# Reading the weights of a one-token decoder layer in longer runs and over all 128 partitions

## Chip, cores, metric

One core of one Trainium2 chip runs the whole layer. The time is the device time of one execution in microseconds (us). The profile's span is some 2 us shorter than that time, because it starts at the first and ends at the last recorded work.

A ratio is the mean time of one kernel's fast runs over that of the other's fast runs of the same rounds, so it is not quite the ratio of the medians that are quoted.

## The reference

```
x = A_x                                        # [4, 1, 576], bf16
h  = x + attention(layernorm(x))               # 32 heads, 16 K/V heads of 128, last 4096 cached keys
out = h + mlp(layernorm(h))                    # gate, up: 576 x 4608, ReLU-gated product, down: 4608 x 576

q = xn @ wq                                    # wq: 576 x 4096
p = softmax(q k^T / sqrt(128)); o = p v        # per batch and head
attention = o.reshape(4, 1, 4096) @ wo         # wo: 4096 x 576
```

Only 4 tokens go through, so every byte of the weights and of the cache is used about once: 134 MB of K and V, 25 MB of weights.

## The kernel before

An own small scheduler keeps a list of operations for each engine and turns dependencies into semaphore waits. All loads are issued by SyncE, in the order in which the data are needed: the first K tile, wq, K and V tiles of 2 MB in a ring of 8 slots, then wo, gate and up, W_down. `place` makes a load wait for the last reader of the SBUF region that it overwrites. PE transposes K, multiplies scores and V; at the end come the wo product, a layernorm with the feature dimension on partitions, the gate/up product, and W_down.

576 features are 4 chunks of 128 and a last chunk of 64. The weights were loaded like this:

```
def add_wq(m):
    ...
    if m < 2:                                   # 256 rows, two per partition: runs of 16 KB
        src = A_wq[m * 256:(m + 1) * 256, :].rearrange("(p r) n -> p (r n)", r=2)
        ...
    else:                                       # the last 64 rows: 64 partitions
        place(("wq", m), off, TILE, "QMM",
              lambda e: e.dma_start(out=arena[0:64, off:off + H * DH], in_=A_wq[512:576, :]), key=f"slot{s}")
...
place(("wo",), WO_OFF, H * D, "WO",             # row h*128+p to partition p: 4096 runs of 1152 B
      lambda e: e.dma_start(out=arena[:, WO_OFF:WO_OFF + H * D].rearrange("p (h n) -> p h n", n=D),
                            in_=A_wo.rearrange("(h p) n -> p h n", p=128)))
...
for c in range(DC):                             # chunks of 128 rows, the last of 64: runs of 9 KB
    w = _dw(c)
    for g, W in ((0, B_W_gate), (1, B_W_up)):
        ...
        place(("gu", g, c), off, F, ("GU", c),
              lambda e, off=off, w=w, W=W, c=c: e.dma_start(out=arena[0:w, off:off + F], in_=W[c * 128:c * 128 + w, :]))
...                                             # W_down: four loads of 9 rows per partition
```

The attention output is turned so that partition p holds element p of every head, which is the order of wo above:

```
pe(("OT", b), lambda e: e.matmul(m_ps[:, 0:32], lhsT=o_sb[:, :], rhs=selw[:, 0, :], start=True, stop=True), ...)
```

Of the kernel before, what the change touches and what calls it, by code (L numbers as in the profile page):

```python
# [6 lines left out]
ALU = mybir.AluOpType  # L7
AX = mybir.AxisListType
FP32 = mybir.dt.float32
BF16 = mybir.dt.bfloat16  # L10

B = 4
D = 576
# [21 lines left out]


def _dw(c):
    return 128 if c < 4 else 64
# [85 lines left out]
def bass_sequential_preLN__sliding_block_cached__glu_gated_reglu__decode_kernel(  # L124
# [12 lines left out]
    with ExitStack() as es:  # L137
# [19 lines left out]
        ind = sb("ind", [128, 32], FP32)  # L157
# [4 lines left out]
        xn_bf = sb("xn_bf", [B, D], BF16)  # L162
        bn = sb("bn", [B, 2, 6], FP32)
        mv = sb("mv", [B, 8], FP32)
        xnT = sb("xnT", [128, DC, 32], BF16)
# [7 lines left out]
        selw = sb("selw", [128, 2, 32], FP32)  # L173
        rL = sb("rL", [128, 32], FP32)
        o_sb = sb("o_sb", [128, 128], FP32)
        oT = sb("oT", [128, H, 32], BF16)
        hnT = sb("hnT", [128, DC, 32], BF16)
        R_sb = sb("R_sb", [128, 2, DC, B], FP32)
# [7 lines left out]
        g_sb = pflat[:, 1152:1152 + 2304].bitcast(FP32)  # L186
        hh = pflat[:, 3456:3456 + 1152]
        hhT = pflat[:, 4608:4608 + 1152]
# [46 lines left out]

        wq_off = []

        def add_wq(m):
            s = ring_slot()
            off = slot0 + s * TILE  # L240
            if m < 2:
                wq_off.extend([off, off + H * DH])
                src = A_wq[m * 256:(m + 1) * 256, :].rearrange("(p r) n -> p (r n)", r=2)
                place(("wq", m), off, TILE, "QMM", lambda e: e.dma_start(out=arena[:, off:off + TILE], in_=src), key=f"slot{s}")
            else:
                wq_off.append(off)
                place(("wq", m), off, TILE, "QMM",
                      lambda e: e.dma_start(out=arena[0:64, off:off + H * DH], in_=A_wq[512:576, :]), key=f"slot{s}")
# [17 lines left out]
        for n, v in enumerate(rest):  # L266
            add_kv("V", v)
            if n == len(rest) - 4:
                place(("wo",), WO_OFF, H * D, "WO",
                      lambda e: e.dma_start(out=arena[:, WO_OFF:WO_OFF + H * D].rearrange("p (h n) -> p h n", n=D),  # L270
                                            in_=A_wo.rearrange("(h p) n -> p h n", p=128)))
        gu_off = {}
        for c in range(DC):
            w = _dw(c)
            for g, W in ((0, B_W_gate), (1, B_W_up)):
                off = GU_OFF + (2 * c + g) * F
                gu_off[(g, c)] = off
                place(("gu", g, c), off, F, ("GU", c),
                      lambda e, off=off, w=w, W=W, c=c: e.dma_start(out=arena[0:w, off:off + F], in_=W[c * 128:c * 128 + w, :]))
        wd_off = []  # L280
        for j in range(4):
            off = WD_OFF + j * WDJ if j < 2 else WO_OFF + (j - 2) * WDJ
            wd_off.append(off)
            place(("wd", j), off, WDJ, "DOWN",
                  lambda e, off=off, j=j: e.dma_start(out=arena[:, off:off + WDJ],
                                                      in_=B_W_down[j * 1152:(j + 1) * 1152, :].rearrange("(p r) n -> p (r n)", p=128)))
# [19 lines left out]
        pool("c_ind0", lambda e: e.memset(ind[:, :], 0.0))  # L306
        prev = "c_ind0"
        for j in range(4):
            pool(f"c_ind{j + 1}", lambda e, j=j: e.affine_select(out=ind[:, :], in_=ind[:, :], pattern=[[-1, 32]],
                                                               compare_op=ALU.not_equal, fill=1.0, base=-32 * j,  # L310
                                                               channel_multiplier=1), [prev])
            prev = f"c_ind{j + 1}"
        pool("c_sel0", lambda e: e.memset(sel4[:, :], 0.0))
        pool("c_sel", lambda e: e.tensor_copy(out=sel4[:, 0:4], in_=ind[:, 0:4]), ["c_sel0", prev])
        IND = prev
        pool("c_oT", lambda e: e.memset(oT[:, :, :], 0.0))
        pool("c_hnT", lambda e: e.memset(hnT[:, :, :], 0.0))
        pool("c_R", lambda e: e.memset(R_sb[:, :, :, :], 0.0))
# [8 lines left out]
        for hf in range(2):  # L327
# [8 lines left out]

        tpv = bankb[6]
        xn_rows = lambda c: (xn_bf[0:B, 512:576] if c == 4 else
                             xn_bf[0:B, c // 2 * 256:c // 2 * 256 + 256].rearrange("b (p r) -> b r p", r=2)[:, c % 2, :])

        def pe_q():
            for c in range(DC):
                w = _dw(c)
                pe(None, lambda e, c=c, w=w: e.transpose(out=tpv[0:w, c * 4:(c + 1) * 4], in_=xn_rows(c),
                                                         identity=ident_b[0:B, 0:B]), ["xn", "c_idb"] if c == 0 else [])
            for c in range(DC):
                w = _dw(c)
                pe("TP1", lambda e, c=c, w=w: e.transpose(out=tpv[0:w, 32 + c * 4:32 + (c + 1) * 4],
                                                          in_=x_bf[0:B, c * 128:c * 128 + w], identity=ident_b[0:B, 0:B]))
            for c in range(DC):  # L350
                w = _dw(c)
                off = wq_off[c]
                for n in range(8):
                    g, bk = n % 4, n // 4
                    pe("QMM", lambda e, c=c, w=w, off=off, n=n, g=g, bk=bk: e.matmul(  # L355
                        bank[4 + bk][32 * g:32 * g + 32, :], lhsT=xnT[0:w, c, :], rhs=arena[0:w, off + n * 512:off + (n + 1) * 512],
# [9 lines left out]
        def dve_q():  # L366
            dve(None, lambda e: e.tensor_copy(out=xnT[:, 0:4, 0:4], in_=tpv[:, 0:16].rearrange("p (c b) -> p c b", b=B)), ["TP1", "c_xnT"])
            dve("xnT", lambda e: e.tensor_copy(out=xnT[0:64, 4, 0:4], in_=tpv[0:64, 16:20]))
            dve(None, lambda e: e.tensor_copy(out=xT[:, 0:4, :], in_=tpv[:, 32:48].rearrange("p (c b) -> p c b", b=B)))
            dve("xT", lambda e: e.tensor_copy(out=xT[0:64, 4, :], in_=tpv[0:64, 48:52]))  # L370
# [112 lines left out]
        def weights(b):  # L483
# [11 lines left out]
            dve(("SEL", b), lambda e: e.tensor_scalar(out=selw[:, 0, :], in0=ind[:, :], scalar1=stat[:, b, 4:5], scalar2=None,  # L495
                                                      op0=ALU.mult), [("W", b), IND])
            dve(("SELL", b), lambda e: e.tensor_scalar(out=selw[:, 1, :], in0=ind[:, :], scalar1=stat[:, b, 4:5],
                                                       scalar2=stat[:, b, 2:3], op0=ALU.mult, op1=ALU.mult), [("EXP", b)])
            pe(("LS", b), lambda e: e.matmul(m_ps[:, 0:32], lhsT=ones_h[:, :], rhs=selw[:, 1, :], start=True, stop=True),
               [("SELL", b), "c_onesh"])  # L500
            dve(("RL", b), lambda e: e.reciprocal(out=rL[:, :], in_=m_ps[:, 0:32]), [("LS", b)])

        def finish_o(b):
            dve(("OEV", b), lambda e: e.tensor_copy(out=o_sb[:, :], in_=o_ps[:, 0:DH]), [("PV", b * KVH + KVH - 1)])  # L504
            pe(("OT", b), lambda e: e.matmul(m_ps[:, 0:32], lhsT=o_sb[:, :], rhs=selw[:, 0, :], start=True, stop=True),
               [("OEV", b), ("SEL", b), ("RL", b)])
            dve(("ONORM", b), lambda e: e.tensor_tensor(out=oT[:, :, b], in0=m_ps[:, 0:32], in1=rL[:, :], op=ALU.mult),  # L507
                [("OT", b), "c_oT", ("RL", b)])
# [43 lines left out]
        act("part1", lambda e: e.copy(out=part[:, 288:576], in_=bank[1][:, 0:288]), ["WO", ("PV", NPAIR - 1)])  # L552
        for c in range(DC):
            w = _dw(c)
            pe("HT", lambda e, c=c, w=w: e.matmul(m_ps[0:w, c * 4:(c + 1) * 4], lhsT=part[:, c * 128:c * 128 + w], rhs=sel4[:, 0:4],
                                                  start=True, stop=True), ["part0", "part1", "c_sel"] if c == 0 else [])
        dve("h1", lambda e: e.tensor_tensor(out=R_sb[:, 0, 0:4, :], in0=m_ps[:, 0:16].rearrange("p (c b) -> p c b", b=B),
                                            in1=xT[:, 0:4, :], op=ALU.add), ["HT", "c_R", "xT"])
        dve("h2", lambda e: e.tensor_tensor(out=R_sb[0:64, 0, 4, :], in0=m_ps[0:64, 16:20], in1=xT[0:64, 4, :], op=ALU.add))
        dve("h3", lambda e: e.tensor_tensor(out=R_sb[:, 1, :, :], in0=R_sb[:, 0, :, :], in1=R_sb[:, 0, :, :], op=ALU.mult),  # L560
            ["h1", "h2"])
        pe("STAT", lambda e: e.matmul(bank[6][:, 0:40], lhsT=ones_d[:, :], rhs=R_sb[:, :, :, :].rearrange("p a c b -> p (a c b)"),
                                      start=True, stop=True), ["h3", "c_onesd", ("OEV", B - 1)])
        dve("s1", lambda e: e.tensor_reduce(out=st2[:, 0:8], in_=bank[6][:, 0:40].rearrange("p (s c b) -> p s b c", s=2, c=DC, b=B),
# [9 lines left out]
        dve("n1", lambda e: e.tensor_tensor(out=tmp5[:, :, :], in0=R_sb[:, 0, :, :], in1=mean_bc, op=ALU.subtract), ["s1"])  # L574
# [85 lines left out]
```

## Time and profile before

| | before |
|---|---|
| median of 3 runs | 398.67 us (398.4 to 399.05) |
| span of the profile | 396.6 us |
| bytes read | 159.58 MB, 402 GB/s over the span |
| PE busy | 65% |

In the views PE is TensorE (matmuls), PEld its loads of weights, DVE VectorE, ACT ScalarE, POOL GpSimd, and SPq SyncE's queue, which issues the loads. A packet is one entry of the DMA records; here it has the size of one run (for wo 4096 packets of 1152 B).

From the page of the kernel before: the busy share of the 16 DMA engines and their rate in 40 equal slices, and the shares of the chain of waits.

```profile
DMA  7999999999999999999999999999999999999993
GB/s 313 385 406 426 418 425 431 422 428 423 423 430 423 425 425 430 430 421 425 425 430 423 425 430 425 429 423 425 423 430 430 410 369 368 426 424 419 229 354 142
...
DMA 61%; PE 25%; SPq 6%; DVE 5%; issue 1%; ACT 1%
```

The DMA row is full from the second slice to the last but one, so the DMA engines bound the kernel, and every stretch in which a full row moves fewer bytes is a loss. The rate row shows them: slices 2 and 3 (385, 406), slices 33 and 34 (369, 368), and the dip to 229 in slice 38. The windows view of the kernel before places them. Its columns are the stretch, its length, the busy time of the five engines with their instructions, the granted clock of TensorE, the DMA share and the rate:

```profile
core 0: us, PE busy (x) PEld busy (x) DVE busy (x) ACT busy (x) POOL busy (x), PEclk, DMA share, GB/s
17.50:20.50 3.00, 1.80 (x16) 0.48 (x16) 0.00 (x0) 0.00 (x0) 0.00 (x0) 0.72 1.14 257
313.00:320.00 7.00, 2.88 (x132) 2.44 (x124) 0.00 (x0) 0.00 (x0) 0.00 (x0) 0.74 1.01 396
322.00:325.00 3.00, 1.90 (x64) 1.63 (x64) 0.00 (x0) 0.00 (x0) 0.00 (x0) 0.50 1.08 391
326.00:329.00 3.00, 0.00 (x0) 0.00 (x0) 0.00 (x0) 0.00 (x0) 0.00 (x0) 0.50 0.60 211
350.00:366.00 16.00, 11.45 (x186) 7.52 (x178) 2.58 (x13) 0.60 (x2) 0.00 (x0) 0.68 1.01 424
367.00:372.00 5.00, 0.67 (x12) 0.23 (x12) 0.00 (x0) 0.00 (x0) 0.00 (x0) 0.84 1.04 225
372.00:379.50 7.50, 2.30 (x24) 0.58 (x24) 0.00 (x0) 0.00 (x0) 0.00 (x0) 0.50 0.99 217
388.30:392.20 3.90, 0.75 (x36) 0.56 (x36) 0.00 (x0) 0.00 (x0) 0.00 (x0) 0.83 0.46 190
```

The stretch at 350 us is the normal rate. Around 19 us come wq's last 64 rows, from 367 to 379.5 us the last 64 rows of gate and up: the DMA share is 1 and the rate is about half (the first window is a little wider than its stretch). From 313 us half of the engines read wo and the others still V tiles, at 396 GB/s; with all 16 on wo, from 322 us, the rate is 391. In 326 to 329 us half of the engines have nothing to do (DMA share 0.60, 9.6 packets in flight). The view of SyncE's own timeline shows that the loads behind wo were issued late:

```profile
305.27 0.39 SPq L270 DMA_DIRECT2D sb_arena<-in_A_wo_dram  x1
305.71 24.04 SPq L233 DMA_DIRECT2D sb_arena<-in_A_v_cache_dram  x3
```

wo is issued at 305.27 us. The three V tiles behind it take 24.04 us to issue. The end, in PE's timeline of the kernel before (the bracket is the idle time before the group and what ended it):

```profile
385.95 2.00 PE L622 MATMUL psb<-sb_arena,sb_pTm 128*32 128x144 bf16 x72
389.62 0.75 PE L622 MATMUL psb<-sb_arena,sb_pTm 128*32 128x144 bf16 x36 [1.67 <-DMA sb_arena<-in_B_W_down_dram]
392.71 1.27 PE L622 MATMUL psb<-sb_arena,sb_pTm 128*32 128x144 bf16 x36 [2.34 <-DMA sb_arena<-in_B_W_down_dram]
```

After the last landing at 392.7 us, 36 matmuls remain. Last, three pieces of the chain of waits in order of time (start, length, what): each ends when the last byte of that load has landed.

```profile
2.54 18.80 DMA sb_arena<-in_A_wq_dram
...
329.14 19.90 DMA sb_arena<-in_A_v_cache_dram
...
356.87 35.79 DMA sb_arena<-in_B_W_down_dram
```

So wq had landed at 21.3 us, the last V tile at 349.0 us and W_down at 392.7 us.

### The profile page before, as it was taken

The page shows a single profiled execution, that of the slowest core. Times are in us where ns is not written, and L with a number is a line of the kernel's source. Part 1 is how long each engine was busy: PE and PEld are TensorE (multiplying, and loading weights), DVE is VectorE, ACT ScalarE, POOL GpSimd, SP SyncE. Part 2 cuts the span into 40 slices and gives each one's busy share as a digit, 9 for nine tenths or more (in the row PEclk, how much of TensorE's full clock was granted, in tenths as well). Part 3 has the DMA queues.
Part 4 walks back from the last instruction along what each step waited for, and adds up shares of the span by engine and source line. Part 5 has one row for each costly group of instructions (what it writes and reads, how often), then busy time and mean ns, then how long its engine had stood idle before and what let it go on. Part 6 is the DMA issues. An engine that isn't in the chain of part 4 may idle for free.

```text
span 396.6 us, 10818 instructions
## 1 busy us (share of the span) xinstructions
PE 259.7 (65%) x5123; PEld 206.2 (52%) x5123; DVE 126.7 (32%) x228; ACT 141.3 (36%) x154; POOL 4.4 (1%) x24
## 2 busy tenths in 40 slices
PE   1647999779677768768677777777774530366153
PEld 1535777558466656557566665666653420343022
DVE  3247555734222334423223444222232100011020
ACT  3305777744344453434333634333350100000010
POOL 4000000000000000000000000000000000000000
PEclk9958999998988888987888889888895555558656
DMA  7999999999999999999999999999999999999993
GB/s 313 385 406 426 418 425 431 422 428 423 423 430 423 425 425 430 430 421 425 425 430 423 425 430 425 429 423 425 423 430 430 410 369 368 426 424 419 229 354 142
DMA packets 15668, 160.28 MB, mean 404 GB/s; under 512 B 1348, under 2 KB 5448, under 8 KB 5448
## 3 DMA queue, kind: packets, MB, share of 16 engines
q1 hardware_dynamic: 15600, 159.59, 97.5%
q8 instruction: 40, 0.66, 0.7%
q14 instruction: 4, 0.03, 0.0%
q10 hardware_dynamic: 24, 0.01, 0.0%
HBM read 159.58 MB, written 0.00 MB: 402 GB/s over the span
## 4 chain that ended last, share of the span: by engine, by line
DMA 61%; PE 25%; SPq 6%; DVE 5%; issue 1%; ACT 1%
DMA sb_arena<-in_A_k_cache_dram 34%; PE psb L397 15%; DMA sb_arena<-in_A_v_cache_dram 13%; DMA sb_arena<-in_B_W_down_dram 9%; SPq L233 6%; DMA sb_arena<-in_A_wq_dram 5%; PE psb L427 4%; PE psb L477 3%; DVE sb_pTm L525 2%; DVE sb_pTm L462 1%; PE psb L547 1%; PE psb L450 1%; ACT sb_p_sb L440 1%; DVE sb_arena L409 0%; PE psb L622 0%
## 5 line engine op out<-in xcount | busy, mean ns | idle before, releaser
L397 PE MATMUL psb<-sb_ident_b,sb_arena 128*128 128x128 bf16 x2048 | 146.7, 238 | 58.3 <-DMA sb_arena<-in_A_k_cache_dram 54.8
L411 ACT COPY sb_arena<-psb 128x1024 bf16<-128x1024 bf16 x128 | 124.9, 1014 | 138.4 <-PE psb L397 138.4
L397 PEld LDWEIGHTS psb<-sb_ident_b,sb_arena 128*128 128x128 bf16 x2048 | 134.9, 108 | 71.8 <-DMA sb_arena<-in_A_k_cache_dram 58.0
L409 DVE COPY sb_arena<-psb 128x1024 bf16<-128x1024 bf16 x128 | 88.0, 690 | 145.8 <-PE psb L397 145.7
L477 PE MATMUL psb<-sb_arena,sb_pTm 128*32 128x128 bf16 x2048 | 46.5, 246 | 36.7 <-DMA sb_arena<-in_A_v_cache_dram 32.5
L477 PEld LDWEIGHTS psb<-sb_arena,sb_pTm 128*32 128x32 bf16 x2048 | 40.5, 111 | 53.8 <-DMA sb_arena<-in_A_v_cache_dram 36.1
L427 PE MATMUL psb<-sb_arena,sb_qTm 128*32 128x512 bf16 x512 | 44.5, 426 | 1.8 <-ACT sb_p_sb L440 1.8
L589 PE MATMUL psb<-sb_arena,sb_hnT 128*32 128x384 bf16 (+1 forms) x120 | 8.7, 437 | 13.9 <-DMA sb_arena<-in_B_W_up_dram 7.3
L552 ACT COPY sb_pTm<-psb 128x288 f32<-128x288 f32 x1 | 0.4, 399 | 44.0 <-PE psb L547 44.0
L504 DVE COPY sb_o_sb<-psb 128x128 f32<-128x128 f32 x4 | 1.2, 292 | 44.3 <-PE psb L477 44.3
L589 PEld LDWEIGHTS psb<-sb_arena,sb_hnT 128*32 128x32 bf16 (+1 forms) x120 | 3.5, 117 | 18.4 <-DMA sb_arena<-in_B_W_up_dram 8.8
L427 PEld LDWEIGHTS psb<-sb_arena,sb_qTm 128*32 128x32 bf16 x512 | 8.0, 96 | 9.5 <-issue 4.1
L462 DVE TENSOR_SCALAR sb_pTm<-psb,sb_par 128x512 bf16<-128x512 bf16 x16 | 9.0, 639 | 6.0 <-PE psb L450 6.0
L440 ACT ACTIVATE sb_p_sb<-psb,sb_stat 128x2048 bf16<-128x2048 f32 x4 | 7.9, 1967 | 5.8 <-DVE sb_stat L436 5.8
L593 ACT ACTIVATE sb_pTm<-psb 128x384 f32<-128x384 f32 x3 | 1.3, 491 | 21.5 <-PE psb L589 21.5
L596 DVE TENSOR_TENSOR sb_pTm<-psb,sb_pTm 128x384 bf16<-128x384 f32 x3 | 1.5, 551 | 21.5 <-ACT sb_pTm L593 21.5
L525 DVE MEMSET sb_pTm<- 128x8192 uint32 x1 | 6.9, 6885 | 1.6 <-issue 1.6
L450 PE MATMUL psb<-sb_ident_b,sb_p_sb 128*128 128x128 bf16 x64 | 5.7, 242 | 2.5 <-DVE sb_oT L507 1.3
L494 ACT ACTIVATE sb_stat<-sb_stat 128x1 f32<-128x1 f32 x4 | 0.8, 203 | 18.0 <-DVE sb_stat L492 18.0
L622 PE MATMUL psb<-sb_arena,sb_pTm 128*32 128x144 bf16 x144 | 4.0, 285 | 4.0 <-DMA sb_arena<-in_B_W_down_dram 4.0
L355 PE MATMUL psb<-sb_arena,sb_xnT 128*32 128x512 bf16 (+1 forms) x40 | 3.9, 516 | 4.1 <-DMA sb_arena<-in_A_wq_dram 3.7
L450 PEld LDWEIGHTS psb<-sb_ident_b,sb_p_sb 128*128 128x128 bf16 x64 | 4.4, 108 | 3.5 <-DVE sb_pTm L462 1.5
(98 smaller groups left out, 66.2 us busy)
## 6 DMA issues: line engine op xcount, KB each, us to landing
sb_arena<-in_A_k_cache_dram SPq DMA_DIRECT2D x32, 2048.0 KB, 32.6
sb_arena<-in_A_v_cache_dram SPq DMA_DIRECT2D x32, 2048.0 KB, 31.0
sb_arena<-in_B_W_down_dram SPq DMA_DIRECT2D x4, 1296.0 KB, 34.1
sb_arena<-in_A_wo_dram SPq DMA_DIRECT2D x1, 4608.0 KB, 29.1
sb_arena<-in_B_W_gate_dram SPq DMA_DIRECT2D x4, 1152.0 KB, 28.7
sb_arena<-in_B_W_up_dram SPq DMA_DIRECT2D x4, 1152.0 KB, 31.0
sb_arena<-in_A_wq_dram SPq DMA_DIRECT2D x2, 2048.0 KB, 14.2
sb_arena<-in_B_W_gate_dram SPq DMA_DIRECT2D x1, 576.0 KB, 36.2
```

Of the source, the lines that this page charges most:

```text
L233: lambda e: e.dma_start(out=arena[:, off:off + TILE], in_=src), key=f"slot{s}")
L397: o = pe(("TRJ", i, j), lambda e, j=j, u=u, t=t: e.transpose(out=bankb[TRB[j]][:, u * 128:(u + 1) * 128], in_=kn[:, t, :], identity=ident_ ...
L409: dve(("EV", i, j), lambda e: e.tensor_copy(out=dst, in_=src), deps)
L411: act(("EV", i, j), lambda e: e.copy(out=dst, in_=src), deps)
L427: o = pe(("QK", i), lambda e, a=a, j=j: e.matmul(bank[4 + u][32 * j:32 * j + 32, :], lhsT=qTm[:, b, 2 * k2 + a, :], rhs=k[:, j, :, :, a], ...
L440: act(("EXP", b), lambda e: e.activation(out=p_sb[:, :].rearrange("p (k a) -> p k a", a=2), in_=bass.AP(tensor=psb, offset=4 * 512, ap=[[4 ...
L450: pe(("PT", b, r), lambda e, tl=tl: e.transpose(out=mb_ps[:, tl * 128:(tl + 1) * 128], in_=p_sb[:, (r * 8 + tl) * 128:(r * 8 + tl + 1) * 128],
L462: dve(("PM", b, r, a), lambda e, dst=dst, src=src, a=a: e.tensor_scalar(out=dst, in0=src, scalar1=par[:, a:a + 1], scalar2=None, op0=ALU.m ...
L477: pe(("PV", i), lambda e, tl=tl, j=j: e.matmul(o_ps[32 * j:32 * j + 32, 0:DH], lhsT=pTm[:, u * 8 + tl, j, k2, :], rhs=v[:, 16 * j + 8 * u ...
L525: dve("c_pTm", lambda e: e.memset(pflat, 0.0))
L589: pe(("GU", c), lambda e, c=c, w=w, g=g, m=m, j=j, lo=lo: e.matmul(bank[3 * g + m][32 * j:32 * j + 32, 0:384], lhsT=hnT[0:w, c, :], rhs=ar ...
L622: pe("DOWN", lambda e, j=j, r=r, n=n, wv=wv: e.matmul(bank[0][32 * n:32 * n + 32, 0:144], lhsT=hhT[:, r * 128 + 32 * j:r * 128 + 32 * j + 32],
```

## The change

The intent is to keep the DMA engines at their full rate over the whole run:

- the last 64 rows of wq, gate and up are cut in two halves of columns and put on 128 partitions, two partitions to a row;
- wo is read with 32 consecutive rows in one partition (36 KB runs), gate and up with two (18 KB runs);
- the activations are laid out to match: four matmuls instead of one turn the attention output, the last chunk of features is duplicated over pairs of partitions and masked by parity, and the layernorm sums count that chunk by half;
- the last load of W_down is cut into 6 and 3 rows, so that fewer matmuls wait for the last bytes.

```diff
+        def rows(W, m):
+            if m < 2:
+                return W[m * 256:(m + 1) * 256, :].rearrange("(p r) n -> p (r n)", r=2)
+            return W[512:576, :].rearrange("r (a n) -> (r a) n", a=2)
...
-                      lambda e: e.dma_start(out=arena[0:64, off:off + H * DH], in_=A_wq[512:576, :]), key=f"slot{s}")
+            place(("wq", m), off, n, "QMM", lambda e: e.dma_start(out=arena[:, off:off + n], in_=rows(A_wq, m)), key=f"slot{s}")
...
-                      lambda e: e.dma_start(out=arena[:, WO_OFF:WO_OFF + H * D].rearrange("p (h n) -> p h n", n=D),
-                                            in_=A_wo.rearrange("(h p) n -> p h n", p=128)))
+                      lambda e: e.dma_start(out=arena[:, WO_OFF:WO_OFF + H * D], in_=A_wo.rearrange("(p r) n -> p (r n)", p=128)))
...
-                      lambda e, off=off, w=w, W=W, c=c: e.dma_start(out=arena[0:w, off:off + F], in_=W[c * 128:c * 128 + w, :]))
+                      lambda e, off=off, n=n, W=W, m=m: e.dma_start(out=arena[:, off:off + n], in_=rows(W, m)))
...
+            for r0, r1 in ((0, 9),) if j < 3 else ((0, 6), (6, 9)):
...
-            pe(("OT", b), lambda e: e.matmul(m_ps[:, 0:32], lhsT=o_sb[:, :], rhs=selw[:, 0, :], start=True, stop=True),
+            for q in range(4):
+                pe(("OT", b), lambda e, q=q: e.matmul(m_ps[:, 0:32], lhsT=selw[:, q, :], rhs=o_sb[:, 32 * q:32 * q + 32],
+                                                      start=(q == 0), stop=(q == 3)),
...
+        dve("n2", lambda e: e.tensor_copy(out=hnT[:, 0:4, 0:4], in_=tmp5[:, 0:4, :]), ["n2a", "c_hnT"])
+        for a in range(2):
+            dve("n3", lambda e, a=a: e.tensor_scalar(out=hnT[:, 4 + a, 0:4], in0=tmp5[:, 4, :], scalar1=par[:, a:a + 1], scalar2=None,
+                                                     op0=ALU.mult), ["n2a", "c_hnT"])
```

(The constants, the transposes of x and the order of the gate/up matmuls are cut.)

## The prediction

> **What bounds it now.** The DMA engines. The page's DMA row is full from 3 to 390 us, at about 425 GB/s; PE is busy 65%. The chain of waits gives 61% to DMA. So the time is the sum of the transfers of the slower engines, plus a start and a tail. Three stretches (windows view) fall below 425 GB/s:
>
> - 17.3 to 20.9 us, 215 GB/s: wq's last 64 rows. Their 8 KB packets take 0.61 us each, as long as a 16 KB packet elsewhere.
> - 313 to 334 us, 390 GB/s, and 211 GB/s in 326 to 329: wo, 4096 packets of 1152 B at 0.051 us.
> - 367 to 379.5 us, 220 GB/s with all 16 engines busy: gate/up's last 64 rows.
>
> At the end, 388 to 392 us runs at 196 GB/s: half the engines are done. From wo on they run some 7 us ahead of the others.
>
> **Why 64 rows cost that much.** [...] the rate halves. It lasts 12.5 us, though 1.18 MB at 215 GB/s is 5.5 us: I think because the two halves of the engines reach these rows at different times, and each visit halves both.
>
> **Costing.** Packet durations fit 8.5 ns plus size/27.2 GB/s (1152 B 0.051, 9216 B 0.347, 16384 B 0.611 us); new sizes are estimated from that fit. Along the late half of the engines, which never idles and ends last:
>
> - wq: 3.5 us at half rate becomes full rate: -1.6 us.
> - wo: 256 packets x 0.051 = 13.1 us per engine becomes 8 rows of 36 KB, 10.9 us: -2.1 us. The hole at 326 to 329 us (SyncE's next issue was held up until 328.5 us behind wo's descriptors) hit the early half, so filling it gains nothing directly.
> - gate/up last rows: -6.2 us.
> - gate/up in 18 KB runs: per engine 64 packets of 9 KB become 32 of 18 KB, 22.2 to 22.0 us: -0.2 us.
> - Last W_down piece is cut 6 + 3 rows, so 12 matmuls remain after the last landing instead of 36 (1.30 us now): -0.8 us; +0.1 us for shorter runs.
>
> Added: four f32 matmul pairs for OT instead of one (about +0.5 us), partd, n2a/n3 and a second STAT matmul (about +1 us) on the PE/DVE chain between the last V and the gate/up matmuls; Pool constants at the start, in its idle time. That chain now ends at 360.9 us; I estimate 358.6 after. The gate/up matmuls then take 7 to 9 us, to about 367; gate/up's last landing falls near 369: still bound by DMA, with 1 to 2 us to spare. So the added work is hidden. W_down's last landing: near 381.8 us.
>
> **Sum:** -11.6 us. Predicted 387.0 us, range 384.8 to 390.5. Faster by over 2% 0.94, within 2% 0.05, slower 0.01.
>
> **What would show it.** No window at 215 GB/s with all engines busy; 4 KB and 4.6 KB packets near 0.16 and 0.18 us; no long SyncE issue behind wo; wo over in about 11 us per engine; 12 matmuls after the last landing; a one-sided DMA tail of 3 to 7 us still there.
>
> **What would make it wrong.** 36 KB runs cut into small pieces or read slower; the half rate coming from something other than the 64 rows; PE and its 0.5 clock becoming the limit after 365 us, which would eat 1 to 3 us; or the early half gaining no lead, which would gain up to 2 us more.

The terms for wq and for gate/up's last rows come from rates in the trace of before (the text's 215 to 220 GB/s, beside 424 in the window at 350 us); that 128 partitions would bring the full rate was the estimate. The sum is -11.6 us; its terms add to -10.8 us, as told at the end.

## The result

| | before | after |
|---|---|---|
| median | 398.6 us (398.4 to 399.05, 4 runs) | 388.63 us (388.57 to 388.7, 4 runs) |
| ratio | | 0.9748, 95% interval 0.9732 to 0.9765 |
| span | 396.6 us | 386.9 us |
| mean rate over the span | 402 GB/s | 412 GB/s |

The kernel is 2.5% faster, 10.0 us. The same lines of the page, of the new kernel:

```profile
DMA  7999999999999999999999999999999999999993
GB/s 307 425 430 432 430 418 427 421 427 425 429 430 422 423 427 427 425 425 425 427 427 427 429 422 420 426 427 429 425 425 427 422 447 420 417 432 425 420 380 123
...
DMA 65%; PE 25%; DVE 5%; issue 1%; ACT 1%; SPq 1%
```

The dips are gone, and the share of DMA in the chain has grown. The windows of the new kernel:

```profile
core 0: us, PE busy (x) PEld busy (x) DVE busy (x) ACT busy (x) POOL busy (x), PEclk, DMA share, GB/s
17.50:20.50 3.00, 1.66 (x24) 0.46 (x24) 0.29 (x1) 0.29 (x1) 0.00 (x0) 1.00 1.03 430
313.00:320.00 7.00, 1.64 (x88) 1.19 (x76) 0.00 (x0) 0.00 (x0) 0.00 (x0) 0.74 1.01 430
326.00:329.00 3.00, 0.00 (x0) 0.00 (x0) 0.00 (x0) 0.00 (x0) 0.00 (x0) 0.50 0.98 415
360.00:370.00 10.00, 7.02 (x100) 3.76 (x104) 0.48 (x4) 0.00 (x0) 0.00 (x0) 0.67 1.00 417
375.10:383.10 8.00, 5.04 (x144) 3.76 (x145) 0.76 (x2) 0.27 (x1) 0.00 (x0) 0.55 0.52 214
```

Around 19 us and in 360 to 370 us, where the last 64 rows now come, the rate is 430 and 417 GB/s. A new thing stands in the last line: for 8 us the DMA share is 0.52. The stretch was 3.9 us long before. Half of the engines have ended their loads by then (8 packets are in flight at 378 us, 16 at 375 us). I call them the early half, the others the late half, and the time in which only the late half still works the tail. SyncE's timeline of the new kernel:

```profile
304.06 0.33 SPq L272 DMA_DIRECT2D sb_arena<-in_A_wo_dram  x1
304.44 1.83 SPq L235 DMA_DIRECT2D sb_arena<-in_A_v_cache_dram  x3
```

The three V tiles behind wo are issued in 1.83 us. PE at the end, new kernel:

```profile
376.20 2.54 PE L650 MATMUL psb<-sb_arena,sb_pTm 128*32 128x144 bf16 x72 [0.34 <-DVE sb_pTm L634]
380.57 1.27 PE L650 MATMUL psb<-sb_arena,sb_pTm 128*32 128x144 bf16 x36 [1.83 <-DMA sb_arena<-in_B_W_down_dram]
382.62 1.61 PE L650 MATMUL psb<-sb_arena,sb_pTm 128*32 128x144 bf16 x36 [0.78 <-DMA sb_arena<-in_B_W_down_dram]
```

The third and fourth W_down pieces wait for DMA (1.83 and 0.78 us idle), so PE isn't the limit. Their last 12 matmuls start at 383.68 us, when the last 3 rows have landed. The chain of waits, new kernel:

```profile
2.52 16.98 DMA sb_arena<-in_A_wq_dram
...
305.66 40.80 DMA sb_arena<-in_A_v_cache_dram
...
356.79 26.84 DMA sb_arena<-in_B_W_down_dram
```

With the landing times of both chains, and the last landing of gate/up (380.61 and 371.27 us, from the PE work that waited for it: the first line is of the kernel before, the second of the new one), the 9.7 us of the span divide like this:

```profile
380.61 1.15 PE L589 MATMUL psb<-sb_arena,sb_hnT 64*32 64x384 bf16 x12 [1.65 <-DMA sb_arena<-in_B_W_up_dram]
371.27 0.14 PEld L617 LDWEIGHTS psb<-sb_arena,sb_hnT 128*32 128x32 bf16 x8 [0.84 <-DMA sb_arena<-in_B_W_up_dram]
```

| stretch | before, ends at | after, ends at | gain in this stretch | predicted |
|---|---|---|---|---|
| to wq landed | 21.34 | 19.50 | 1.84 | 1.6 |
| to the last V landed (contains wo) | 349.04 | 346.46 | 0.74 | 2.1 |
| to gate/up landed | 380.61 | 371.27 | 6.76 | 6.4 |
| to W_down landed | 392.66 | 383.63 | -0.31 | -0.1 |
| to the end of the span | 396.6 | 386.9 | 0.7 | 0.8 |

### The profile page after: what moved, and what is told of

Read it like the earlier page. It is cut to its first block, busy times and chain, and to the rows that moved or that the text cites. A ratio compares the mean times of both kernels' runs of the same rounds, so it can differ in the third digit from the quotient of the medians.

```text
span 386.9 us, 10877 instructions
## 1 busy us (share of the span) xinstructions
PE 263.6 (68%) x5149; PEld 211.2 (55%) x5149; DVE 128.7 (33%) x233; ACT 141.5 (37%) x154; POOL 7.2 (2%) x29
## 4 chain that ended last, share of the span: by engine, by line
DMA 65%; PE 25%; DVE 5%; issue 1%; ACT 1%; SPq 1%
DMA sb_arena<-in_A_k_cache_dram 43%; PE psb L414 16%; DMA sb_arena<-in_A_v_cache_dram 11%; DMA sb_arena<-in_B_W_down_dram 7%; DMA sb_arena<-in_A_wq_dram 4%; PE psb L444 4%; PE psb L494 3%; DVE sb_pTm L547 2%; DVE sb_pTm L479 1%; ACT sb_p_sb L457 1%; PE psb L569 1%; DVE sb_stat L451 1%; PE psb L525 0%; PE psb L467 0%; SPq L235 0%
## 5 line engine op out<-in xcount | busy, mean ns | idle before, releaser
L494 PEld LDWEIGHTS psb<-sb_arena,sb_pTm 128*32 128x32 bf16 x2048 | 41.2, 113 | 48.9 <-DMA sb_arena<-in_A_v_cache_dram 31.9
L617 PE MATMUL psb<-sb_arena,sb_hnT 128*32 128x384 bf16 x120 | 9.3, 488 | 4.7 <-DMA sb_arena<-in_B_W_up_dram 2.3
L617 PEld LDWEIGHTS psb<-sb_arena,sb_hnT 128*32 128x32 bf16 x120 | 4.3, 133 | 9.0 <-DMA sb_arena<-in_B_W_up_dram 3.6
L650 PE MATMUL psb<-sb_arena,sb_pTm 128*32 128x144 bf16 x144 | 5.3, 324 | 3.1 <-DMA sb_arena<-in_B_W_down_dram 2.6
L467 PE MATMUL psb<-sb_ident_b,sb_p_sb 128*128 128x128 bf16 x64 | 4.9, 220 | 2.9 <-DVE sb_pTm L479 1.2
L650 PEld LDWEIGHTS psb<-sb_arena,sb_pTm 128*32 128x32 bf16 x144 | 3.8, 138 | 4.4 <-DMA sb_arena<-in_B_W_down_dram 3.9
L525 PE MATMUL psb<-sb_o_sb,sb_selw 128*128 128x32 f32 x32 | 5.1, 310 | 1.6 <-DVE sb_o_sb L523 1.6
L525 PEld LDWEIGHTS psb<-sb_o_sb,sb_selw 128*128 128x128 f32 x32 | 4.7, 225 | 2.5 <-DVE sb_o_sb L523 2.5
```

The costliest lines, as they stand in the source:

```text
L467: pe(("PT", b, r), lambda e, tl=tl: e.transpose(out=mb_ps[:, tl * 128:(tl + 1) * 128], in_=p_sb[:, (r * 8 + tl) * 128:(r * 8 + tl + 1) * 128],
L494: pe(("PV", i), lambda e, tl=tl, j=j: e.matmul(o_ps[32 * j:32 * j + 32, 0:DH], lhsT=pTm[:, u * 8 + tl, j, k2, :], rhs=v[:, 16 * j + 8 * u ...
L525: pe(("OT", b), lambda e, q=q: e.matmul(m_ps[:, 0:32], lhsT=selw[:, q, :], rhs=o_sb[:, 32 * q:32 * q + 32], start=(q == 0), stop=(q == 3)) ...
L617: pe(("GU", c), lambda e, g=g, m=m, j=j, lo=lo, c=c: e.matmul(bank[3 * g + m][32 * j:32 * j + 32, 0:384], lhsT=hnT[:, c if c < 4 else 4 + ...
L650: pe("DOWN", lambda e, j=j, r=r, n=n, wv=wv: e.matmul(bank[0][32 * n:32 * n + 32, 0:144], lhsT=hhT[:, r * 128 + 32 * j:r * 128 + 32 * j + 32],
```

## The experiments

The theory to test: the DMA stream of the engines that end last is the time; 64-partition loads halve it, for longer than their own bytes need; wo's short runs cost a little; and work added to PE is hidden. Every kernel starts from the new one, and "slower" or "faster" is against its 388.63 us. Comparing medians of different chips is a risk, since the new kernel itself did not run in the experiments. ot_twice, which was expected not to differ, ran on another chip in 388.66 us, but it is itself a test. The traces support the comparison better: fewer than 14 packets are in flight from 375.1 to 375.4 us on in the new kernel, dma_only, ot_twice, less_fetch and more_fetch2 alike, on different chips. By the ratios the times on two of the chips come out 0.7 to 0.9 us lower against the new kernel (early64 +5.5 us, early128 +2.1, more_fetch2 +0.6, less_fetch -2.6).

### wo back to short runs

```diff
-                      lambda e: e.dma_start(out=arena[:, WO_OFF:WO_OFF + H * D], in_=A_wo.rearrange("(p r) n -> p (r n)", p=128)))
+                      lambda e: e.dma_start(out=arena[:, WO_OFF:WO_OFF + H * D].rearrange("p (h n) -> p h n", n=D),
+                                            in_=A_wo.rearrange("(h p) n -> p h n", p=128)))
...   (and the one OT matmul of before, with its selector, so that the result stays right)
```

> The new kernel with wo alone taken back to 4096 runs of 1152 B (with the old order of the attention output, so the result stays right). Theory A (my corrected costing: in the trace of before 17.3 of these packets are in flight on 16 engines, so one costs an engine 47 ns and not its recorded 51 ns; only the late half of the engines counts): 1.1 us slower than the new kernel, so ratio to before near 0.9775; the SyncE issue behind wo is held up for some 20 us again, a hole of about 3 us at half rate appears, and the one-sided tail shrinks from 7.7 us to about 4 us. Theory B (the costing on record, 51 ns each): 2.1 us slower, ratio 0.980. Theory C (the hole costs as well): 3.5 us or more slower, ratio 0.9835 or more.

Measured: 389.63 us, correct, ratio 0.9778 (0.976 to 0.9795). That is 1.0 us slower: theory A. SyncE's timeline of this kernel shows the blocked issue again:

```profile
303.99 24.18 SPq L236 DMA_DIRECT2D sb_arena<-in_A_v_cache_dram  x3
```

The DMA records show the hole (at 326 us 9 packets are in flight, not 16) and a one-sided tail of 3.7 us, where the new kernel has 8.05 us. So filling the hole moved half of the engines forward and moved the last ones only by the 0.9 us of wo's short runs (last load at 384.1 and 383.2 us): the hole of 3 us became 4 us more of tail.

### gate/up's last 64 rows back on 64 partitions

```diff
-                      lambda e, off=off, n=n, W=W, m=m: e.dma_start(out=arena[:, off:off + n], in_=rows(W, m)))
+                      lambda e, off=off, n=n, W=W, m=m, w=w: e.dma_start(out=arena[0:w, off:off + n],
+                                                                         in_=rows(W, m) if m < 2 else W[512:576, :]))
...   (n = F and w = 64 for m == 2; an unduplicated chunk hn64[0:64] of the normalized h as lhsT for these rows)
```

> The new kernel with only the last 64 rows of gate and up read into 64 partitions in 9 KB runs, as before. Theory A (64-partition loads halve all engines, and the two halves of the engines reach them some 7 us apart, so the half rate lasts about 12 us): 6 to 7 us slower than the new kernel, ratio near 0.991; 12 to 13 us at 215 GB/s. Theory B (64-partition loads run at half rate for their own bytes only): 2.8 us slower, ratio near 0.982, 5.5 us at 215 GB/s. Theory C (the half rate is not due to the 64 partitions): no change, ratio 0.975.

Measured: 396.13 us, correct, ratio 0.9937 (0.9921 to 0.9953): 7.5 us slower, of the 10.0 us that the whole change gained. Theory A, a little beyond its 7 us. The windows of this kernel (same columns as before) show two visits, with a recovery between them:

```profile
361.00:365.00 4.00, 3.28 (x48) 1.62 (x40) 0.00 (x0) 0.00 (x0) 0.00 (x0) 0.65 1.04 234
366.00:370.00 4.00, 0.17 (x6) 0.00 (x0) 0.00 (x0) 0.00 (x0) 0.00 (x0) 1.00 1.00 345
372.00:376.00 4.00, 2.95 (x36) 1.05 (x36) 0.00 (x0) 0.00 (x0) 0.00 (x0) 0.50 0.99 209
```

In 361 to 365 us, eight engines of the early half read the 64 rows while the others still read 128-partition rows; in 372 to 376 us it is the other way round. The sizes of the packets in flight show this. Both times the rate halves for all (234 and 209 GB/s): in the first visit the others' packets of 18432 B take about 1.25 to 1.4 us instead of 0.69, in the second W_down's packets of 10368 B about 0.76 us instead of 0.389. The lag between the halves is larger here than before the change (8 against 4 us), which fits that undoing costs 7.5 us while the change gained 6.76 us in this stretch; no run varies the lag alone.

### The same 64 rows at the start, where all engines are in step

```diff
+        for g, W in ((0, B_W_gate), (1, B_W_up)):            # after wq; early64:
+            P.dma("sync", ("L", "xtra", g), lambda e, g=g, W=W: e.dma_start(out=pflat[0:64, g * F:(g + 1) * F], in_=W[512:576, :]), f"d_xtra{g}")
                                                              # early128 instead:
+            ...  e.dma_start(out=pflat[:, g * F // 2:(g + 1) * F // 2], in_=rows(W, 2)) ...
-                dve("c_pTm", lambda e: e.memset(pflat, 0.0))
+                dve("c_pTm", lambda e: e.memset(pflat, 0.0), [("L", "xtra", 0), ("L", "xtra", 1)])
```

That they are in step there can be read from the new kernel's records: wq's last 128 packets start from 17.5 us on, 16 of them within 0.3 us, and the last 16 end between 18.86 and 19.04 us.

> The new kernel plus 1.18 MB of extra loads right after wq at the start, when all engines are in step: gate's and up's last 64 rows, read once more into 64 partitions (never used). Theory A (in step, the half rate lasts once, for these bytes alone): at 215 GB/s 5.5 us, with a run-off of about 0.8 us, so 5.5 to 6.3 us slower than the new kernel, and 2.8 to 3.5 us slower than early128. Theory B (64-partition loads always cost what they cost at the end, 12 us at half rate): 9 us or more slower than the new kernel and 6 to 7 us slower than early128.

> The same extra 1.18 MB, read into 128 partitions in 4.6 KB runs. Both theories: 2.8 us slower than the new kernel (1.18 MB at 425 GB/s), ratio to before near 0.982; no stretch at half rate.

Measured: early64 394.95 us (ratio 0.9887, 0.987 to 0.9903), early128 391.43 us (ratio 0.9801, 0.9785 to 0.9817), both correct: 6.3 and 2.8 us slower. The same 1.18 MB, 64 against 128 partitions, cost 3.5 us more in step and 7.5 us more out of step. Theory A holds. One window of early64, and the same of early128 (same columns):

```profile
19.50:24.00 4.50, 1.24 (x16) 0.57 (x16) 1.48 (x9) 0.59 (x1) 0.00 (x0) 1.00 1.04 215
```

```profile
19.50:24.00 4.50, 2.08 (x16) 0.91 (x16) 0.93 (x4) 0.59 (x1) 0.00 (x0) 0.50 1.05 438
```

### wq's last 64 rows back on 64 partitions

```diff
-            place(("wq", m), off, n, "QMM", lambda e: e.dma_start(out=arena[:, off:off + n], in_=rows(A_wq, m)), key=f"slot{s}")
+            place(("wq", m), off, n, "QMM", lambda e: e.dma_start(out=arena[0:w, off:off + n], in_=rows(A_wq, m) if m < 2 else A_wq[512:576, :]), key=f"slot{s}")
...   (n = H * DH and w = 64 for m == 2, and xnT's last chunk on 64 partitions)
```

> The new kernel with only wq's last 64 rows read into 64 partitions, as before. If the DMA stream of the whole run is shifted by what the stretch at 17 to 21 us loses: 1.6 us slower than the new kernel, ratio near 0.979. Rival: the loss at the start is absorbed later, because K tiles queue up for PE until about 100 us: under 0.4 us, ratio 0.975 to 0.976.

Measured: 390.34 us, correct, ratio 0.9799 (0.978 to 0.9817): 1.7 us slower. What is lost in the first 21 us is still missing at the end; in the page of the new kernel the DMA row is full in between. The rival falls.

### The last W_down piece in one load

```diff
-            for r0, r1 in ((0, 9),) if j < 3 else ((0, 6), (6, 9)):
+            for r0, r1 in ((0, 9),):
```

> The new kernel with the last W_down piece loaded whole (9 rows per partition). After the last landing 36 matmuls remain instead of 12: 0.7 to 0.8 us slower than the new kernel, ratio near 0.9767, the stream itself ending 0.1 us earlier. Rival: nothing, because the matmuls of the first six rows cannot run before the last landing either; ratio 0.975.

Measured: 389.25 us, correct, ratio 0.9768 (0.975 to 0.9785): 0.6 us slower, close to the expected 0.7. The interval alone would not tell it from the new kernel; that all four runs lie between 389.15 and 389.35 us does.

### Added PE work doubled

```diff
+            for rep in range(2):
                 for q in range(4):
                     pe(("OT", b), ...)
```

> The new kernel with the four matmuls of the last step of attention done twice (same result): about 1.9 us more on the chain of PE and VectorE between the last V and the gate/up matmuls at the half clock. If that chain is hidden behind the weights' DMA with 1 to 2 us to spare, as the trace of the new kernel shows: 0 to 0.4 us slower than the new kernel, ratio 0.975 to 0.976. Rival (PE already bounds the end): 1.5 to 2 us slower, ratio 0.979 or more.

Measured: 388.66 us, correct, ratio 0.973 (0.9714 to 0.9747): no slower. The half clock of the expectation is in the new kernel's trace: around these matmuls, at 348.8 to 350.8 us, the granted clock is 0.50. The largest added piece on the chain of PE and VectorE is hidden; the smaller ones (partd, n2a/n3, STAT) were not doubled.

### Which part of 64 partitions is the cost: the partitions, or the number of engines that write them

```diff
+                for p0 in (0, 1, 2, 3, 32, 33, 34, 35):      # 8 loads of 8 rows, 4 partitions apart, per matrix
+                    make = lambda e, off=off, n=n, W=W, p0=p0: e.dma_start(
+                        out=arena[p0:p0 + 29:4, off:off + n], in_=W[512 + p0:512 + p0 + 29:4, :])
...   (the rest as in gu64)
```

> The last 64 rows of gate and up go to partitions 0 to 63 again in 9 KB runs, as in gu64, but by eight loads of 8 rows each per matrix, the rows of one load 4 partitions apart[...]. Theory A[...]: no stretch at 215 GB/s. Then the eight engines carry the whole 1.18 MB, 16 packets of 0.347 us each instead of 16 of 0.178 us: if they are the early half, the late half is relieved of 2.85 us and the kernel is 2.5 to 3 us faster than the new kernel (ratio near 0.968), the one-sided tail shrinking from 7.7 to about 2 us; if they are the late half, it is 2.7 us slower (ratio near 0.982) and the tail grows to 13 us. Theory B (64 partitions run at half rate whichever engines write them): about 7.5 us slower like gu64, ratio near 0.994.

That a load of 8 rows uses eight engines was assumed; the trace fits it (below).

Measured: 391.29 us, correct, ratio 0.9817 (0.9799 to 0.9836): 2.7 us slower than the new kernel and 4.8 us faster than gu64, with the same rows on the same 64 partitions. The windows (same columns):

```profile
360.00:372.00 12.00, 6.75 (x108) 3.47 (x108) 0.59 (x5) 0.00 (x0) 0.00 (x0) 0.78 1.00 420
380.00:385.80 5.80, 2.70 (x111) 2.32 (x104) 0.00 (x0) 0.00 (x0) 0.00 (x0) 0.79 0.14 57
```

The half rate is gone (420 GB/s in the first line), so 64 partitions as such do not cost it. The trace fits eight engines: 96 of the 128 packets of 9 KB run up to six at a time, the other 32 two at a time, which is 16 for each of eight engines. So it is shown that loading these rows on fewer engines avoids the half rate, but not by what mechanism, nor why 128-partition loads on other engines halve as well in gu64. The records name no engine.

My guess that these eight engines are either the early half or the late half was wrong, although the time fits the second. In the records six packets of 9 KB are in flight at 362 to 364 us and two from 368 us on: six of the eight engines belong to the early half and two to the late one. At the end two engines alone work until 385.8 us (57 GB/s in the second line above), and they make the 2.7 us.

### Where the lag of half of the engines comes from

First the loads alone, without any compute:

```diff
-                owner[blk] = reader
+                owner[blk] = ("L",) + name        # a slot waits only for the load before it
...   (all operations of PE, VectorE, ScalarE and GpSimd removed; x copied to out)
```

> The loads of the new kernel in the same order and sizes, each slot waiting only for the earlier load into it; no compute at all, the output is wrong on purpose (a copy of x). Measures the floor of the stream and where the lead of half the engines comes from. Theory A (half of the engines move each packet a little slower, 0.62 against 0.61 us): a one-sided tail of 4 us or more stays, and the stream ends within 3 us of the new kernel's. Theory B (the lead comes from the instruction fetches, 40 of 16 KB that share the engines with the loads, and there are almost none here): the tail is under 2 us and the stream ends 4 to 7 us earlier than the new kernel's.

Measured: 380.54 us, ratio 0.9526 (0.951 to 0.9542). It passed the comparison with the reference although it computes nothing, because x is most of the output. The page of this kernel, rate in 40 slices and the loads' queue:

```profile
GB/s 308 425 436 424 432 424 432 426 432 426 432 424 432 424 432 426 432 426 431 426 429 429 424 434 422 434 424 434 422 432 426 432 443 424 418 429 429 429 417 268
...
q1 hardware_dynamic: 11384, 159.59, 99.0%
```

The last slice moves 268 GB/s where the new kernel's moves 123: there is no one-sided tail. The last 16 packets of the loads end between 375.5 and 376.6 us, about 1 us apart: no half is late. In the new kernel the early half begins to run out at 375.1 us as well, and the late half is done at 383.2 us. So something that comes with the compute delays half of the engines by 8 us and the others not at all.

The instruction fetches are the candidate: on its queue q8, of the kind "instruction", the new kernel has 40 packets of 16 KB for 10,877 instructions, one for each 272, and dma_only, with 113 instructions, has no such queue. Each stands in the records in place of a load's packet, for 1.07 us on average. Two more kernels change their number:

```diff
+                for _ in range(2 if tl < 7 else 0):          # more_fetch2; more_fetch: 5
+                    pe(None, lambda e: e.matmul(bank[6][0:32, 256:257], lhsT=ident_b[:, 0:32], rhs=ident_b[:, 0:1],
+                                                start=True, stop=True, skip_group_check=True))
```

> The new kernel with 2240 tiny matmuls of one column added among those of the V tiles, into an unused column; PE has a third of its time free, and the result stays the same. They add about 4480 PE instructions, 41% more, so some 17 more instruction fetches of 16 KB besides the 40. Theory A (the lead of half the engines comes from the fetches, which fall on the other half and cost it 42.7 us of packets plus 20 us of slowed loads for 40, 1.57 us each): the late half loses 17 x 1.57 / 8 = 3.3 us more, so 3.3 us slower than the new kernel (ratio near 0.983) and a one-sided tail of about 11 us. Theory B (the lead comes from compute engines using SBUF, not from the fetches): under 0.7 us slower, tail unchanged at 7 to 8 us. Theory C (PE becomes the limit): 5 us or more slower, with the DMA row of the page no longer full.

Measured: 418.63 us (416.39 to 420.49), correct, ratio 1.0501 (1.0467 to 1.0535). The fetches rose to 57 as counted, but PE became the limit (theory C), as the page's DMA row shows:

```profile
DMA  7999999999999999999999999989999139999990
```

The stream ran dry in slices 32 and 33 (57 and 114 GB/s), and the halves came back into step there. This run says nothing about the lag. The smaller dose:

> As more_fetch, with 896 tiny matmuls instead of 2240, so that PE should not become the limit; the result stays the same. 1792 more PE instructions, by the count of more_fetch (17 more fetches for 4480) 7 more fetches. Theory A (the fetches fall on the half that ends last, at 1.57 us each over eight engines): 1.4 us slower than the new kernel (ratio near 0.978), tail about 9 us. Theory B (the lead has another cause in the compute): under 0.4 us slower, tail as before at 7 to 8 us. Theory C (PE still limits): 3 us or more slower, DMA row with slices under 9.

Measured: 390.12 us, correct, ratio 0.9762 (0.9739 to 0.9785): 1.5 us slower. And fewer instructions:

```diff
-            for tl in range(8):
+            for tl in range(2):                              # less_fetch, V product
```

> The new kernel with only two of the eight key groups of each V tile multiplied (wrong on purpose; all loads stay). 1536 fewer matmuls, 3072 fewer PE instructions, so about 12 fewer fetches, 28 instead of 40. Theory A (the fetches make the late half late): 2.4 us faster than the new kernel, ratio near 0.969, tail near 5.5 us. Theory B (PE reading SBUF slows the loads): only the packet durations of the loads would change; theory D (nothing but PE time changes, and PE is not the limit): no change, ratio 0.974 to 0.976, tail 7 to 8 us.

Measured: 386.98 us (wrong), ratio 0.9684 (0.9661 to 0.9707): 1.65 us faster, less than the 2.4 us expected. The queue of the instruction fetches (packets, MB, share of the span of 16 engines) in the new kernel, in more_fetch2 and in less_fetch:

```profile
q8 instruction: 40, 0.66, 0.7%
```

```profile
q8 instruction: 47, 0.77, 0.8%
```

```profile
q8 instruction: 28, 0.46, 0.5%
```

Together, with times taken from the DMA records:

| kernel | fetches of 16 KB | fewer than 14 packets in flight from | last load ends | tail |
|---|---|---|---|---|
| dma_only | 0 | 375.1 us | 376.6 us | 1.5 us |
| less_fetch | 28 | 375.3 us | 381.5 us | 6.2 us |
| new kernel | 40 | 375.1 us | 383.2 us | 8.05 us |
| more_fetch2 | 47 | 375.2 us | 384.65 us | 9.45 us |

By the ratios, more_fetch2 and less_fetch are 0.8% apart, 3.1 us, as by the medians. The early half does not move; the late half moves by (384.65 - 376.6) / 47 = 0.17 us for each fetch, 1.4 us of engine time if eight engines share them evenly.

The records do not name the engines, but they hold more. In these records a packet usually starts within some 4 ns of the end of the one before it on its engine, so the packets can be linked, by times and by the known order of loads, into 16 chains of equal length, one for each engine. This linking is an inference, but it comes out without a remainder. In the new kernel the 40 fetches fall on eight chains in turn, five on each; these end at 382.8 to 383.2 us, and the eight chains without a fetch at 375.0 to 377.3 us. The other kernels tell fetches from compute as a whole, within one execution each:

| kernel | fetches on a chain | chains | their loads end |
|---|---|---|---|
| less_fetch | 3 | 4 | 379.8 to 380.0 us |
| less_fetch | 4 | 4 | 381.3 to 381.5 us |
| more_fetch2 | 5 | 1 | 383.0 us |
| more_fetch2 | 6 | 7 | 384.3 to 384.7 us |

So one more fetch makes its engine 1.4 to 1.5 us later: about 1.07 us for the fetch, and about 0.5 us because the load's packet behind it takes some 1.1 us instead of 0.61. It also tells why less_fetch gained 1.65 us and not 2.4: its last chains lost one fetch of five. Why the fetches go to these eight engines stays open, and whether PE itself waited for them was not looked at.

## Why the prediction was right, and where it was not

- **What bounds the kernel**: right. The DMA row is full in both kernels, the loads without compute already take 380.54 us, and doubling the largest piece of the added PE work costs nothing (388.66 against 388.63 us).
- **gate/up's last 64 rows, -6.2 us**: right. The stretch gained 6.76 us, of which 0.2 us were expected from longer runs; undoing these rows alone costs 7.5 us. The reason for its length held too: in step the 64 partitions cost 3.5 us more than 128, out of step 7.5 us. What halves the rate is not shown; the runs show only that with eight engines instead of sixteen the same 64 partitions do not halve it (gu_k8, 420 GB/s).
- **wq, -1.6 us**: right, 1.84 us in the trace and 1.7 us by undoing it.
- **wo, -2.1 us**: mis-sized. Undoing it costs 1.0 us, and the stretch that contains it gained 0.74 us. The failed step is "256 packets x 0.051 = 13.1 us per engine". The recorded duration of a short packet isn't the spacing of packets: some 17.3 of them are in flight on 16 engines, and at 391 GB/s (all 16 engines on wo, 322 to 325 us) an engine starts one each 1152 B x 16 / 391 GB/s = 0.047 us, which makes 12.1 us per engine against 10.9 us for eight 36 KB packets (1.367 us each). For 16 KB packets the overlap is too small to matter (16.1 in flight on 16 engines from 100 to 200 us), so the fit over sizes was good at one end only. The windows view, from which the prediction quoted 390 GB/s, had the right rate.
- **The hole behind wo gains nothing directly**: right. With it the tail is 3.7 us, without it 8.05 us.
- **W_down's last piece, -0.8 + 0.1 us**: 0.7 us in the span's last stretch, 0.6 us by undoing it.
- **Added PE work hidden**: right, though under-costed. The chain before the gate/up matmuls ended at 360.66 us, not at 358.6 us: the four OT matmul pairs took 1.91 us instead of 0.64 us, +1.3 us where +0.5 us was assumed. Most of the rest of the delay is the last V tile, which landed about 1.1 us later than the wo term had it.
- **"Sum: -11.6 us"**: wrong as a sum. The listed terms add to -10.8 us, that is 387.8 us. So half of the miss of 1.6 us is addition. Of the terms, wo's is off by 1.0 us or more, the others by 0.4 us or less each, in both directions.
- **A tail of 3 to 7 us still there**: right in kind, 8.05 us in size. The prediction had no cause for it; the runs give one, the instruction fetches, with the linked chains as the closest evidence.

The four parts undone one at a time cost 1.0 + 7.5 + 1.7 + 0.6 = 10.8 us, against 10.0 us for the whole. I read the surplus as interaction: with the hole, the halves are 4 us apart instead of 8 us, and the out-of-step cost of the 64 rows is smaller. No run undoes two parts at once.

No version beats the new kernel with a right result. What the runs leave is the tail: at 8 us on half of the engines, an even share would, by estimate (half of 8.05 us), end the stream up to 4 us earlier. Fewer PE instructions shorten it (less_fetch: 28 fetches and 6.2 us, against 40 and 8.05 us), but only the wrong kernel had fewer; giving the late engines less data needs to know which they are.

## What to carry to other kernels

In a kernel with a full DMA row, look for stretches where the row is full and the rate is half: here a load into partitions 0 to 63 that was spread over all engines (gu64) slowed every other load in flight with it, twice where the engines weren't in step (234 and 209 GB/s); cut into loads of 8 rows (gu_k8) it did not (420 GB/s). Take the cost of short runs from the rate over a window, not from the durations of single packets, because the packets overlapped here (17.3 of 1152 B in flight on 16 engines). Count only the engines that end last: here filling the hole of the others lengthened the tail from 3.7 to 8.05 us, and the last load ended only 0.9 us earlier.
